# Down weights with 14 adjacent rows in each partition, gate and up read at step 14 to match, in a four-block decode kernel

## The chip, the cores and the metric

The kernel runs on one core of a Trainium2 chip, as one launch. The metric is device time in microseconds. Engines are named as the profile names them: PE is TensorE (matmuls), PEld its loads of the stationary operand, DVE is VectorE, ACT ScalarE, POOL GpSimd, SP SyncE, whose queue issues nearly all transfers here.

## The reference

One token for each of four batch rows passes through attention, a feed-forward block, and the same two again with the same weights. Sizes: model width 512, 32 query heads and 8 key and value heads of width 128, 4096 cached positions, hidden width F = 1792 = 14 x 128, all in bf16.

```python
def _A_ref(x, k_cache, v_cache, wq, wo):
    q = (x @ wq) split into heads
    p = softmax(q . k * Dh ** -0.5)
    return (p . v, heads joined) @ wo

def _B_ref(x, w_gate, w_up, w_down):
    return (_gelu(x @ w_gate) * (x @ w_up)) @ w_down

x = x + _A_ref(_layernorm(x), A_k_cache, A_v_cache, A_wq, A_wo)
x = x + _B_ref(_layernorm(x), B_w_gate, B_w_up, B_w_down)
x = x + _A_ref(_layernorm(x), A_k_cache, A_v_cache, A_wq, A_wo)
x = x + _B_ref(_layernorm(x), B_w_gate, B_w_up, B_w_down)
```

(The first function is cut to what it computes.) The hidden vector of 1792 is summed over in the last product, so any order of its elements gives the same result as long as gate, up and down use the same one.

## The kernel before, in words

All weights stay in SBUF. `load_rest` (L139) loads them once, on SyncE's queue: the output weights `wo_sb` in four parts, gate `wg_sb` and up `wu_sb` in one DMA each, down `wd_sb` in three (L147, chunks 0 to 5, 6 to 10 and 11 to 13). The model dimension lies on the partitions in gate and up, four blocks of 128 (`KD`), each with 1792 columns side by side. The hidden dimension lies on the partitions in down, 14 chunks (`KF`): hidden element c x 128 + p is in partition p, chunk c, so each run of memory that a DMA reads for a partition is one row of 512 bf16, 1 KB.

The order of the work is written out by hand. Batch rows follow one another. For each row, `attend` (or `attend_first`) runs the first layer's attention, and interleaves it with the second layer's attention of the row before. Then `dense` (`dense_first` for row 0, L1109) does the row's first feed-forward block, and after it the queries for its second attention are made. All four rows' second feed-forward block comes at the end, in `dense_last` (L1157). Keys are loaded into fixed tiles, by `load` and `load_pairs` (L472, L481), once the scores that read the tile before are done; values go through a ring of eight slots (`pump`, L634), each loaded again when TensorE has used it. One V tile is 512 KB. In `dense`, `prev.fill()` puts the use of one such V tile of the row before between the matrix products; TensorE works in the order of the program, so what stands behind a product waits for it.

Gate and up are multiplied in three ways:

- `dense_first` calls `ffn_in` (L387): the weights are the stationary operand, 56 blocks of 128 x 128 for each matrix (14 chunks by 4 blocks of the model dimension), and the vector streams past them. They pass through the helper `mac` (L246). `busy(n)` (L443) adds n filler matmuls of 512 columns on `wg_sb`, whose results nobody reads: six between gate and up, four after up, two at each boundary between parts of the down weights. The down product is L246 again, 56 matmuls.
- `dense` calls `ffn_rows` (L289), which goes through `streamed` and `streamed_part` (L274): the vector is the stationary operand, 32 equal columns, and the weights stream past it. Each of the four blocks is cut into four quarters j of 14 x 32 columns, whose results go to PSUM partitions 32j to 32j + 31: 16 matmuls of 448 columns for each matrix. `turn_rows` (L280) then transposes 32 x 32 blocks on VectorE, after which hidden element c x 128 + 32j + n stands in partition 32j + n, column c.
- `dense_last` does the same with the four rows' vectors as stationary operand (`rows_of`, L1166), for gate and then for up. The results are transposed (L1211 and L1216), shifted, scaled (L1212, L1213, with the root from GpSimd in L181), passed through GELU and multiplied (L1215, L1217, L1219); 56 matmuls with the down weights follow (L1205), then the sum with the residual (L1228) and four small DMAs out (L1232).

The pattern that cuts the columns into quarters is the same in both streamed ways:

```python
blocks = w.rearrange("p (c j n) -> p j c n", j=QD, n=QS)
```

with QD = 4 and QS = 32, so the inner 32 columns n are adjacent in memory. `streamed` is also used for the queries (16 matmuls of 512 columns) and for the down product (56 of 128).

Of the kernel before, what the change touches and what calls it, by code (L numbers as in the profile page):

```python
# [15 lines left out]
P = 128  # L16

LN_EPS = 1e-5
QD = 4
QS = P // QD  # L20
# [13 lines left out]
def kernel(  # L34
# [21 lines left out]
    KD = D // P  # L56
    KF = F // P
# [42 lines left out]
    xb = state.tile([P, KD, 2 * RUN], BF16, name="xb")  # L100
# [18 lines left out]
    def acc(shape, name):  # L119
        t = ps_ac.tile([P, 512], FP32, name=name, tag="acc")  # L120
        n = 1
        for s in shape:
            n *= s
        if len(shape) == 1:
            return t[:, :n]
        return t[:, :n].rearrange("p (a b) -> p a b", b=shape[1])

    def wide(v):
        n = v.shape[-1]
        return v.unsqueeze(1).broadcast_to([P, WIDE // n, n])  # L130
# [8 lines left out]
    def load_rest():  # L139
        n = Hq // 4  # L140
        for i in range(4):
            dq.dma_start(out=wo_sb[:, i * n:(i + 1) * n], in_=wo_dram[:, i * n:(i + 1) * n])  # L142
        dq.dma_start(out=wg_sb[:], in_=B_w_gate.rearrange("(k p) n -> p k n", p=P))  # L143
        dq.dma_start(out=wu_sb[:], in_=B_w_up.rearrange("(k p) n -> p k n", p=P))
        wd_dram = B_w_down.rearrange("(k p) n -> p k n", p=P)
        for lo, hi in zip(WD_PARTS, WD_PARTS[1:]):
            dq.dma_start(out=wd_sb[:, lo:hi], in_=wd_dram[:, lo:hi])  # L147

# [17 lines left out]
    def apart(w_sb, shape, at=0):  # L166
        n = shape[0] * shape[1]
        return (w_sb[:, at].bitcast(FP32)[:, :n].rearrange("p (a b) -> p a b", b=shape[1]))

    def stats(b0, nb):  # L170
        st = ps_sm.tile([P, nb, 2], FP32, name="st", tag="sm")
        for i in range(nb):
            b = b0 + i
            for k in range(KD):
                nc.tensor.matmul(st[:, i], lhsT=xb[:, k, b:b + 1].broadcast_to([P, P]),
                                 rhs=xb[:, k, b:B + 1:B - b],
                                 start=k == 0, stop=k == KD - 1, skip_group_check=True)
        return st
# [66 lines left out]
    def mac(dst, lhsT, rhs, first, last):  # L245
        nc.tensor.matmul(dst, lhsT=lhsT, rhs=rhs, start=first, stop=last, skip_group_check=True)  # L246
# [11 lines left out]
                mac(q[:, i], wq_sb[g][:, k, i * Dh:(i + 1) * Dh],  # L258
                    rhs(k) if nb > 1 else wide(rhs(k)), k == 0, k == KD - 1)

    def streamed(name, n, steps):


        full = acc([n, WIDE], name)
        streamed_part(full, steps, range(len(steps)))
        return full

    def streamed_part(full, steps, part):
        flat = full.rearrange("p c r -> p (c r)")
        for i in part:  # L270
            x, w = steps[i]
            blocks = w.rearrange("p (c j n) -> p j c n", j=QD, n=QS)
            for j in range(QD):
                nc.tensor.matmul(flat[j * QS:(j + 1) * QS], lhsT=x.broadcast_to([P, WIDE]),  # L274
                                 rhs=blocks[:, j], start=i == 0, stop=i == len(steps) - 1,
                                 skip_group_check=True)
# [10 lines left out]
        return streamed("q", HG, q_steps(b, g))  # L287

    def ffn_rows(b, w_sb, name):  # L289
        return streamed(name, KF, [(xb[:, k, b:b + 1], w_sb[:, k]) for k in range(KD)])  # L290

    def down_rows(H_bf):
        return streamed("y2", KD, [(H_bf[:, c, :1], wd_sb[:, c]) for c in range(KF)])
# [35 lines left out]
    def nothing(t):  # L329
        nc.scalar.copy(out=t, in_=qb[:, 0:1].broadcast_to([P, t.shape[1]]))  # L330
# [46 lines left out]
    def add_x(b0, nb, y):  # L377
        bs = slice(b0, b0 + nb)
        nc.vector.tensor_tensor(out=xb[:, :, bs], in0=XX[:, bs].rearrange("p b k -> p k b"),  # L379
                                in1=y, op=ALU.add)  # L380
# [6 lines left out]
    def ffn_in(rhs, w_sb, name):  # L387
        g = acc([KF, WIDE], name)
        for c in range(KF):
            for k in range(KD):  # L390
                mac(g[:, c], w_sb[:, k, c * P:(c + 1) * P], wide(rhs(k)), k == 0, k == KD - 1)
        return g

    def shifts(scr, mr, i):
# [762 lines left out]
    def dense_last(y, full):  # L1157
        up = acc([KF, WIDE], "u")
        nothing(up.rearrange("p c r -> p (c r)"))

        def rows_of(w_sb, full):
            flat = full.rearrange("p c r -> p (c r)")
            for k in range(KD):
                blocks = w_sb[:, k].rearrange("p (c j n) -> p j c n", j=QD, n=QS)
                for j in range(QD):
                    nc.tensor.matmul(flat[j * QS:j * QS + B], lhsT=xb[:, k, :B],  # L1166
                                     rhs=blocks[:, j], start=k == 0, stop=k == KD - 1,
                                     skip_group_check=True)
            return flat

        add_x(0, B, y)
        st = stats(0, B)
        add_y(0, B, y)
        ss, mean = st[:, :, 0], st[:, :, 1]
        shape = [KF, B]
        ln = small.tile([P, 3, B], FP32, name="ln", tag="ln")
        msq, own, rstd = ln[:, 0], ln[:, 1], ln[:, 2]
        t = [apart(wq_sb[0], shape, i) for i in range(2)]

        def shift(i):  # L1180
            nc.vector.tensor_tensor(out=t[i], in0=cols(cs_f[:, i], KF, B), in1=rows(mean, KF, B),
                                    op=ALU.mult)

        xlo = wq_sb[1][:, 0, :KD * B].rearrange("p (k b) -> p k b", b=B)
        nc.vector.tensor_tensor(out=xlo, in0=XX.rearrange("p b k -> p k b"),
                                in1=xb[:, :, :B], op=ALU.subtract)
        nc.scalar.activation(out=msq, in_=mean, func=ACT.Square)
        nc.vector.tensor_scalar(out=rstd, in0=ss, scalar1=1.0 / D, scalar2=LN_EPS,
                                op0=ALU.mult, op1=ALU.add)
        shift(0)  # L1190
        nc.vector.tensor_tensor(out=rstd, in0=rstd, in1=msq, op=ALU.subtract)
        inv_root(rstd, rstd)
        shift(1)

        g_rows = rows_of(wg_sb, full)
        u_rows = rows_of(wu_sb, up)
        xr = ps_sm.tile([P, P], FP32, name="xr", tag="sm")
        yo = ps_sc.tile([P, P], FP32, name="yo", tag="sc")
        zero = qb[:, 0:1].broadcast_to([P, P])
        for clear in (xr, yo):  # L1200
            nc.tensor.matmul(clear[:], lhsT=zero, rhs=zero, start=True, stop=True,
                             skip_group_check=True)

        def row(to, k, lhsT, rhs):
            nc.tensor.matmul(to[k * QS:k * QS + B], lhsT=lhsT, rhs=rhs, start=False, stop=True,  # L1205
                             skip_group_check=True)

        for x in (xb[:], xlo):
            for k in range(KD):
                row(xr, k, x[:, k, :B], ident_bf[:])  # L1210
        nc.vector.transpose(out=g_rows, in_=g_rows)  # L1211
        nc.vector.tensor_tensor(out=t[0], in0=full[:, :, :B], in1=t[0], op=ALU.subtract)  # L1212
        nc.vector.tensor_tensor(out=t[0], in0=t[0], in1=rows(rstd, KF, B), op=ALU.mult)  # L1213
        sq = apart(wq_sb[0], shape, 2)
        nc.scalar.activation(out=sq, in_=t[0], func=ACT.Gelu_apprx_tanh)  # L1215
        nc.vector.transpose(out=u_rows, in_=u_rows)  # L1216
        nc.vector.tensor_tensor(out=t[1], in0=up[:, :, :B], in1=t[1], op=ALU.subtract)  # L1217
        H_bf = wq_sb[1][:, 1, :KF * B].rearrange("p (c b) -> p c b", b=B)
        nc.vector.tensor_tensor(out=H_bf, in0=t[1], in1=sq, op=ALU.mult)  # L1219
        nc.vector.scalar_tensor_tensor(out=msq, in0=rstd, scalar=1.0, in1=hmask, op0=ALU.mult,  # L1220
                                       op1=ALU.mult, accum_out=own[:, :1])
        xs = apart(wq_sb[0], [1, P], 3)[:, 0]
        nc.scalar.copy(out=xs, in_=xr[:])
        for c in range(KF):
            for k in range(KD):
                row(yo, k, H_bf[:, c, :], wd_sb[:, c, k * P:(k + 1) * P])
        xo = pep.tile([P, P], BF16, name="xo", tag="pe")
        nc.vector.scalar_tensor_tensor(out=xo[:], in0=yo[:], scalar=own[:, :1], in1=xs,  # L1228
                                       op0=ALU.mult, op1=ALU.add)
        rows_out = out.flatten_outer_dims()  # L1230
        for k in range(KD):
            (nc.sync, nc.scalar)[k % 2].dma_start(out=rows_out[:, k * P:(k + 1) * P],  # L1232
                                                  in_=xo[k * QS:k * QS + B, :])
# [8 lines left out]
    for b in range(B):  # L1242
# [21 lines left out]
        else:  # L1264
            if b == B - 1:
# [7 lines left out]
                rest, steps = acc([HG, WIDE], "q"), q_steps(b, gy)  # L1273
# [33 lines left out]
        else:  # L1307
            y, full = attend_last(q_bf, norm, prev, late[3 * NT:])
# [32 lines left out]
```

## Time and profile before

| what | value |
|---|---|
| time, median of 3 runs | 275.38 us (273.44 to 275.9) |
| profiled execution, its own time | 271.11 us |
| its span, first to last instruction | 269.2 us |
| mean granted TensorE clock | 0.854 |
| busy: PE, DVE, ACT | 190.0, 174.7, 64.2 us |
| bytes moved | 103.08 MB, 102.50 of them from HBM |
| L274 gate and up, 128x448, 48 matmuls each | 3.6 and 2.8 us busy |
| L1166 gate and up, 128x448, 16 matmuls each | 0.9 us busy each |
| L246 gate and up, 56 matmuls each | 1.7 and 1.6 us busy |

The profile records one execution. Matmuls overlap: the duration of one includes its way through the array, so a group's time in the timeline, from its first start to its last end, says more than a mean times a count. The granted clock is the share of full speed that TensorE was given in a stretch. The chain of work that ended last runs back from the last instruction through what released each step.

### The profile page before, as it was taken

What the parts mean: (1) busy time and instruction counts of PE and PEld (TensorE: products, weight loads), DVE (VectorE), ACT (ScalarE), POOL (GpSimd) and SP (SyncE); (2) the same over time, 40 slices, a digit from 0 to 9 for tenths busy, and PEclk for the clock granted to TensorE, in tenths of its full rate; (3) what the DMA queues carried; (4) which work ended last, traced back from release to release, by engine and by line L of the source; (5) the groups of instructions that cost most, each with busy time, mean ns of one, the idle gap of its engine ahead of it and who ended that gap; (6) DMA issues with size and microseconds to landing.
All of it is one profiled execution on the core that took longest, in us unless ns stands there. A gap on an engine that the chain in (4) does not pass through costs nothing.

```text
span 269.2 us, 8883 instructions
## 1 busy us (share of the span) xinstructions
PE 190.0 (71%) x3943; PEld 113.8 (42%) x3943; DVE 174.7 (65%) x428; ACT 64.2 (24%) x125; POOL 2.7 (1%) x8
## 2 busy tenths in 40 slices
PE   1395255634597896968869969687788786788893
PEld 1333133633364443544426335454354354453561
DVE  3394952130124799875676999566759995768863
ACT  1001000100404412030422610304137113044640
POOL 2000000000000000000000000000000000000001
PEclk9999559555599798687897997889979979799999
DMA  6999999999993999999999999999999999999940
GB/s 244 421 417 421 418 420 416 413 382 402 411 360 100 419 415 418 420 418 416 402 386 417 417 420 417 416 422 416 412 417 415 417 419 417 416 391 386 417 159 3
DMA packets 32430, 103.08 MB, mean 383 GB/s; under 512 B 2692, under 2 KB 8584, under 8 KB 32392
## 3 DMA queue, kind: packets, MB, share of 16 engines
q1 hardware_dynamic: 32368, 102.51, 95.1%
q8 instruction: 31, 0.51, 0.7%
q14 instruction: 7, 0.06, 0.1%
q10 hardware_dynamic: 24, 0.01, 0.0%
HBM read 102.50 MB, written 0.00 MB: 381 GB/s over the span
## 4 chain that ended last, share of the span: by engine, by line
DMA 51%; DVE 21%; PE 17%; SPq 6%; issue 2%; ACT 1%; DVEq 0%; ACTq 0%
DMA v_t<-in_A_v_cache_dram 29%; DMA kp<-in_A_k_cache_dram 13%; DVE kp L488 10%; PE sc L531 7%; DMA wu_sb<-in_B_w_up_dram 5%; DMA kp<-in_A_v_cache_dram 4%; SPq L142 4%; PE so L712 2%; DVE pe L541 2%; DVE q L280 2%; DVE qb L316 1%; PE ot L779 1%; PE y L246 1%; PE q L274 1%; SPq L143 1%
## 5 line engine op out<-in xcount | busy, mean ns | idle before, releaser
L488 DVE STREAM_TRANSPOSE kp<-kp 128x1024 f32<-128x1024 f32 x64 | 74.0, 1206 | 0.2 <-issue 0.2
L531 PE MATMUL sc<-kp,qb 128*32 128x512 bf16 x512 | 66.6, 449 | 7.5 <-DVE qb L316 2.5
L779 PE MATMUL ot<-pe,v_t 128*128 128x32 bf16 x1120 | 35.3, 181 | 14.4 <-DMA v_t<-in_A_v_cache_dram 12.4
L779 PEld LDWEIGHTS <-v_t 128*128 128x128 bf16 x1120 | 33.1, 99 | 24.2 <-DMA v_t<-in_A_v_cache_dram 15.9
L531 PEld LDWEIGHTS <-qb 128*32 128x32 bf16 x512 | 21.3, 102 | 42.2 <-issue 23.1
L553 ACT ACTIVATE pe<-sc,nl 128x512 bf16<-128x512 f32 x8 | 5.5, 687 | 84.9 <-DVE pe L550 67.2
L583 PE MATMUL x<-pe,ident_bf 128*32 128x128 bf16 x192 | 6.0, 255 | 15.1 <-DVE pe L561 15.0
L583 PEld LDWEIGHTS <-ident_bf 128*32 128x32 bf16 x256 | 5.6, 107 | 18.9 <-issue 17.1
L541 DVE TENSOR_REDUCE pe<-sc 128x1 f32<-128x512 f32 x12 | 8.3, 689 | 7.9 <-PE sc L531 7.9
L720 DVE STREAM_TRANSPOSE so<-so 128x256 f32<-128x256 f32 (+1 forms) x19 | 11.1, 584 | 3.2 <-PE so L712 3.1
L712 PE MATMUL so<-v_t,pe 128*32 128x256 bf16 x192 | 10.2, 341 | 2.8 <-ACT pe L586 1.4
L246 PE MATMUL y<-OT_bf,wo_sb 128*128 128x32 bf16 x192 | 7.3, 190 | 6.8 <-DMA wo_sb<-in_A_wo_dram 6.7
L246 PEld LDWEIGHTS <-wo_sb 128*128 128x128 bf16 x256 | 8.6, 102 | 8.0 <-DMA wo_sb<-in_A_wo_dram 7.1
L586 ACT CAST pe<-x 128x512 bf16<-128x512 f32 x12 | 7.0, 585 | 20.3 <-PE x L583 20.3
L712 PE MATMUL so<-v_t,pl 128*32 128x256 bf16 x192 | 9.7, 283 | 2.9 <-DMA v_t<-in_A_v_cache_dram 2.6
L379 DVE TENSOR_TENSOR xb<-XX,y 128x4 bf16<-128x4 f32 (+1 forms) x9 | 1.6, 173 | 14.2 <-PE y L246 14.1
L246 PE MATMUL q<-xb,wq_sb 128*128 128x5 bf16 (+1 forms) x192 | 5.4, 170 | 7.3 <-DMA wq_sb<-in_A_wq_dram 7.3
L561 DVE STREAM_TRANSPOSE pe<-pe 128x512 bf16<-128x512 bf16 x12 | 8.4, 697 | 3.2 <-ACT pe L553 3.2
L616 DVE TENSOR_TENSOR OT_bf<-ot,rden 128x8 bf16<-128x8 f32 (+1 forms) x20 | 3.0, 156 | 11.1 <-PE ot L779 11.0
L360 PE MATMUL yr<-wo_sb,OT_bf 128*2 128x512 bf16 (+1 forms) x96 | 10.2, 494 | 0.0
L310 PE MATMUL qe<-q_bf,ident_bf 128*32 128x16 bf16 x256 | 4.4, 175 | 8.2 <-DVE q_bf L299 6.3
L712 PEld LDWEIGHTS <-pe 128*32 128x32 bf16 x208 | 6.1, 113 | 8.2 <-issue 3.8
(148 smaller groups left out, 229.6 us busy)
## 6 DMA issues: line engine op xcount, KB each, us to landing
v_t<-in_A_v_cache_dram SPq DMA_DIRECT2D x97, 512.0 KB, 8.9
kp<-in_A_k_cache_dram SPq DMA_DIRECT2D x40, 512.0 KB, 12.4
kp<-in_A_k_cache_dram SPq DMA_DIRECT2D x12, 1024.0 KB, 8.3
wq_sb<-in_A_wq_dram SPq DMA_DIRECT2D x2, 2048.0 KB
wo_sb<-in_A_wo_dram SPq DMA_DIRECT2D x4, 1024.0 KB, 11.4
wq_sb<-in_A_v_cache_dram SPq DMA_DIRECT2D x3, 1024.0 KB, 11.2
wg_sb<-in_B_w_gate_dram SPq DMA_DIRECT2D x1, 1792.0 KB
wu_sb<-in_B_w_up_dram SPq DMA_DIRECT2D x1, 1792.0 KB
```

The source lines that it names most:

```text
L142: dq.dma_start(out=wo_sb[:, i * n:(i + 1) * n], in_=wo_dram[:, i * n:(i + 1) * n])
L246: nc.tensor.matmul(dst, lhsT=lhsT, rhs=rhs, start=first, stop=last, skip_group_check=True)
L360: nc.tensor.matmul(self.rows[j:j + x.shape[1]], lhsT=x, rhs=wo_sb[:, i], start=self.n < QD, stop=True, skip_group_check=True)
L488: nc.vector.transpose(out=words, in_=words)
L531: nc.tensor.matmul(sc[s * QS:(s + 1) * QS], lhsT=qb[:, w0:w0 + 2 * W], rhs=kt[:, :, be // 2, :, be % 2], start=(t == 0 and be == 0), stop= ...
L541: nc.vector.tensor_reduce(out=m, in_=sc.rearrange("p c j -> p (c j)"), axis=AX.X, op=ALU.min if norm else ALU.max)
L561: nc.vector.transpose(out=flat, in_=flat)
L583: nc.tensor.matmul(x[a * QS:(a + 1) * QS, s], lhsT=ident_bf[:, s * QS:(s + 1) * QS], rhs=pT[:, a], start=True, stop=True, skip_group_check ...
L586: nc.scalar.copy(out=pe, in_=x.rearrange("p s t c h -> p (s t c h)"))
L712: nc.tensor.matmul(ps[d, :NW * QS], lhsT=x[:, w:w + NW].rearrange("p c h -> p (c h)"), rhs=v[:, i:i + NW, d], start=first and i == 0, stop ...
L720: nc.vector.transpose(out=flat, in_=flat)
L779: nc.tensor.matmul(self.ot[:, s % 2], lhsT=v[:, i, :], rhs=wide(pe[:, s, t * CH + i, :]), start=(done == 0 and i == 0), stop=(done == NT - ...
```

## The change

Down is read so that partition p holds the 14 adjacent rows 14p to 14p + 13; chunk c is row 14p + c. One partition's part of a load is then one run of memory of 6, 5 or 3 KB, in place of as many separate rows of 1 KB. The three DMAs and their bytes stay.

Gate and up are loaded as before. Their columns are read in the matching order: hidden element 14p + c must come out in partition p, column c. In `ffn_in` the block of 128 columns becomes every fourteenth column from c on; in `streamed_part` and `rows_of` a quarter is 32 x 14 adjacent columns, and the stream takes the inner 32 at a step of 14 (28 bytes). The queries and the down product keep the old order. Numbers and sizes of matmuls, and everything after them, are the same.

```diff
-        wd_dram = B_w_down.rearrange("(k p) n -> p k n", p=P)
+        wd_dram = B_w_down.rearrange("(p k) n -> p k n", p=P)
         for lo, hi in zip(WD_PARTS, WD_PARTS[1:]):
             dq.dma_start(out=wd_sb[:, lo:hi], in_=wd_dram[:, lo:hi])
...
-    def streamed(name, n, steps):
+    in_chunks = dict(order="p (c j n) -> p j c n", j=QD, n=QS)
+    in_rows = dict(order="p (j n c) -> p j c n", j=QD, n=QS)
+
+    def blocks_of(w, order, **sizes):
+        return w.rearrange(order, **sizes)
+
+    def streamed(name, n, steps, layout=in_chunks):
         full = acc([n, WIDE], name)
-        streamed_part(full, steps, range(len(steps)))
+        streamed_part(full, steps, range(len(steps)), layout)
         return full
 
-    def streamed_part(full, steps, part):
+    def streamed_part(full, steps, part, layout=in_chunks):
         flat = full.rearrange("p c r -> p (c r)")
         for i in part:
             x, w = steps[i]
-            blocks = w.rearrange("p (c j n) -> p j c n", j=QD, n=QS)
+            blocks = blocks_of(w, **layout)
             for j in range(QD):
                 nc.tensor.matmul(flat[j * QS:(j + 1) * QS], lhsT=x.broadcast_to([P, WIDE]),
                                  rhs=blocks[:, j], start=i == 0, stop=i == len(steps) - 1,
...
     def ffn_rows(b, w_sb, name):
-        return streamed(name, KF, [(xb[:, k, b:b + 1], w_sb[:, k]) for k in range(KD)])
+        return streamed(name, KF, [(xb[:, k, b:b + 1], w_sb[:, k]) for k in range(KD)], in_rows)
...
         for c in range(KF):
             for k in range(KD):
-                mac(g[:, c], w_sb[:, k, c * P:(c + 1) * P], wide(rhs(k)), k == 0, k == KD - 1)
+                mac(g[:, c], w_sb[:, k, c::KF], wide(rhs(k)), k == 0, k == KD - 1)
         return g
...
             for k in range(KD):
-                blocks = w_sb[:, k].rearrange("p (c j n) -> p j c n", j=QD, n=QS)
+                blocks = blocks_of(w_sb[:, k], **in_rows)
                 for j in range(QD):
                     nc.tensor.matmul(flat[j * QS:j * QS + B], lhsT=xb[:, k, :B],
```

## The prediction

> **What bounds the kernel now.** I read the page's rate row first, then the chain of work that ended last, then single stretches by windows and by timeline. The rate row gives the GB/s of 40 slices of 6.73 us.
>
> ```profile
> GB/s 244 421 417 421 418 420 416 413 382 402 411 360 100 419 415 418 420 418 416 402 386 417 417 420 417 416 422 416 412 417 415 417 419 417 416 391 386 417 159 3
> ...
> DMA 51%; DVE 21%; PE 17%; SPq 6%; issue 2%; ACT 1%; DVEq 0%; ACTq 0%
> ```
>
> Nearly every slice is at 416 to 421, so bytes set the time: 102.5 MB at 417 GB/s are 246 us of the span of 269.2. The rest is the hole in slice 13 and the last ten microseconds, where no transfer is left. Only there does a slower engine lengthen the run one for one. The hole, by windows of 2 us (last two columns: share of the DMA engines, GB/s):
>
> ```profile
> 59.00:61.00 2.00, 1.06 (x32) 1.07 (x32) 0.00 (x0) 0.00 (x0) 0.00 (x0) 0.50 1.09 386
> 67.00:69.00 2.00, 0.00 (x0) 0.00 (x0) 0.54 (x3) 1.45 (x3) 0.00 (x0) 0.50 1.02 416
> 75.00:77.00 2.00, 1.94 (x47) 1.20 (x43) 0.72 (x4) 0.00 (x0) 0.00 (x0) 1.00 1.06 370
> ...
> 83.00:85.00 2.00, 2.00 (x36) 1.09 (x40) 0.05 (x1) 0.86 (x1) 0.00 (x0) 1.00 0.00 0
> ```
>
> The windows at 59 and 75 carry the output and down weights, rows of 1 KB: 370 to 386 GB/s. The window at 67 carries gate, rows of 3.5 KB: 416. At 83 nothing moves. The chain shows what closes the hole:
>
> ```profile
> 60.01 14.43 DMA wu_sb<-in_B_w_up_dram
> 74.48 1.60 PE u L246 x56
> ...
> 76.85 0.23 DVE words L433
> 77.22 0.75 PE y L246 x24
> ...
> 82.99 2.10 PE sc L531 x27
> ```
>
> It is a run of computation from the landing of up to the first scores. SyncE's next load waits for those (L481 for PE sc L531, once for 10.5 us in its waits). In the timeline, the matmuls that the change makes stepped (start, duration, then what):
>
> ```profile
> 127.57 1.69 PE L274 MATMUL g<-wg_sb,xb 128*32 128x448 bf16 x16
> ...
> 237.41 0.94 PE L274 MATMUL g<-wg_sb,xb 128*32 128x448 bf16 x16
> ```
> ```profile
> 261.67 0.93 PE L1166 MATMUL gr<-wg_sb,xb 128*4 128x448 bf16 x16
> ...
> 262.43 0.93 PE L1166 MATMUL u<-wu_sb,xb 128*4 128x448 bf16 x16
> ...
> 262.65 0.67 DVE L1211 STREAM_TRANSPOSE gr<-gr 128x448 f32<-128x448 f32 x1 [0.19 <-PE gr L1166]
> ...
> 263.67 0.22 DVE L1213 TENSOR_TENSOR wq_sb<-wq_sb,ln 128x56 f32<-128x56 f32 x1
> 263.80 0.66 DVE L1216 STREAM_TRANSPOSE u<-u 128x448 f32<-128x448 f32 x1
> ```
>
> Sixteen go as four rounds of four column quarters running together. At granted clock 1.00 up starts 0.76 us after gate, so a round takes 190 ns. The group at 127.57 ran at 0.50: less the 0.58 us of its last matmul, 1.69 us are three rounds of 370 ns. The group at 261.67 stands in the open tail.
>
> **The change, part by part.** The sum is made on the profiled execution, 271.11 us (span 269.2, 1.9 around it). It lies 1.6% under the median of 275.38 and below the lowest of the three runs, 273.44; I add the difference to the median.
>
> *Down weights loaded (L147).* 1.835 MB in rows of 6, 5 and 3 KB in place of 1 KB; three DMAs as before. At 416 in place of 370 to 386 GB/s they take 4.4 us, not 4.8 to 5.0: 0.4 to 0.6 us sooner. Who waits? The timeline has the last twelve L246 matmuls on them at 79.25, 0.07 us behind the filler ahead of them (two L443 matmuls of 0.22 us from 78.75); the first 24 start 0.14 us after L433 ends. So at most 0.15 us is on the chain. The 1 MB of K behind them lands sooner into a hole whose end is set by scores. SyncE gets through L147 sooner and then stands in L481's wait; nothing is issued sooner. Price: -0.1, between -0.6 (all of it on the path) and 0.
>
> *Gate and up as weights at step 14 (L391, first row of the batch).* Twice 56 loads of 128x128. They run at 27 ns each at 70.15 (1.68 us, granted clock 0.50) and at 26 at 74.48 (1.58 us, 1.00). So they don't follow the array's clock, and a read that only reached half speed would be hidden at full clock. Lower end 0. Upper end: the slowest 128x128 load in the trace, the f32 one of L566, 188 ns against 96 in its own row; twice the pace would be 1.5 us for each matrix. Both are on the chain into the hole: gate's ends at 71.84, six fillers run to 74.39, up lands then. No slack, so +2.9. I take +0.1, by the pair at 70.15 and 74.48, which is the same instruction.
>
> [...] No run here shows a step of 14 in a weight load.
>
> *Gate and up as streams at step 14, rows two to four (L274).* Neighbouring elements lie 28 bytes apart. No row of before reads that way. The nearest stepped row is the scores' (L531, step 2): 32 matmuls of 512 in 2.00 us at 245.65, against 1.05 for 16 unit-step ones (L274 q). Less the last matmul (0.39 and 0.38) these are seven rounds of 230 ns and three of 223: 3%. From there to step 14 I have bounds only. Lower: no cost, 190 ns a round. Upper: the four quarters no longer run together. One stream of 512 takes 0.22 us in the L443 fillers (four in 1.02 us with the drain), so a quarter of 448 takes 188 and a round 750 ns, four times. Between lies a read at half speed, as the group at 127.57 shows it: 370 ns, twice. I take twice. Step 2 already costs a little where a read with speed to spare would cost nothing, which speaks against zero; that quarters would queue behind one another is something the unit-step rows, four abreast, give no sign of.
>
> At twice, each matrix takes 0.75 us more: 1.5 us in each of three rows of the batch. TensorE is in order, so V tiles behind it are consumed and their slots reissued later. The cover is the queue: a V tile issued at 127.49 lands 5.7 us later (chain), one at 232.60 after 7.84. So 1.5 us leave the DMAs fed. Yet the windows around 132 to 139 sag to 356 to 401 GB/s with the queue at its shortest, so I put +0.2 there for all three. If the cover were gone it would be 3 x 1.5 = +4.5.
>
> *The same in the tail (L1166).* Gate's last result comes 0.75 us later and the vector chain from L1211 on moves with it: L1216 from 263.80 to 264.55. Up starts 0.75 later and takes 0.75 more: its end goes from 263.36 to 264.86, past 264.55, so L1216 starts at about 264.9. Cost +1.1. At four times: 263.36 + 4.5 = 267.86, so +4.1. At no cost 0.
>
> Sum: -0.1 + 0.1 + 0.2 + 1.1 = +1.3 us; 271.1 becomes 272.4, and the median 276.7.
>
> [...]
>
> **The rivals.** *No penalty.* Stepping streams for nothing leaves -0.1: 275.3 us. For it: only 3% at step 2.
>
> *Quarters take turns* (the other side: slower). Four times a round: tail +4.1; in each middle row 2 x 2.2 = 4.5 us, against a cover of 5.7. The reissues at 237 to 242 would come just as the queue runs out, about 1 us lost per row, so +3; loads +0 to +2.9. Together +7 to +10, middle 283.9. It decides from about three times on, where the tail alone gives 263.36 + 3.0 - 263.8 = +2.6. For it: four streams each touching a new place on every element. Against: no row has it.
>
> *The weight loads slow down, streams or not.* 1.5 to 2.9 us in the hole with twice the pace, above that if they fall to the pace of L566, 131 ns (two matmuls in 0.39 us at 228.00, the second 0.26 of it), which is 56 x 105 ns = +5.9 for each matrix: 277 to 287. Against: the pace's indifference to the clock.
>
> *Half speed, but the cover fails*: +1.3 and up to +4.3, 278 to 281. *Faster*: the whole down load on the path is 0.6 us, 0.2%; more than 1% would need something the trace does not show.
>
> **How the numbers follow.** About 1%, 2.75 us, is what a measurement of this kernel can tell from no change. Half speed 0.38 (276.7) and no penalty 0.20 (275.3) are within it: 0.58. Turns 0.24, slow weight loads 0.10 and the failed cover 0.05 are slower: 0.39. Faster 0.03. The likeliest one's own range is 275.5 to 278. The range goes down to 274.0, no penalty with the scatter of the runs, and up to the middle of the turns at 284.0; left out are the upper half of the turns (0.12), the top of the loads (0.04) and faster (0.03).
>
> **What would show it.** In the tail, L1166 at 1.7 us for each matrix at clock 1.00: half speed; 0.93 no penalty; 3.2 turns. L1216 should follow the end of up, not L1213. L246 on gate and up in the hole should stay near 1.6 us. The down weights' windows should read near 416 GB/s with the hole wider on its early side. The slices around 135 and 240 tell whether the cover held. I am wrong if the tail's length doesn't move, or if the hole ends later than 11 us after up's landing.

## The result and the profile after

The changed kernel takes 291.59 us (median of 6 runs, 290.24 to 293.11), the one before 274.01 us in the same count of runs (271.82 to 275.9). The ratio is 1.0676, 95% interval 1.0635 to 1.0717: 18.5 us slower. (It is taken over fast runs alone, so it is not quite the quotient of these medians.) I had forecast 276.7 with 284.0 as the upper end. The profiled execution after took 290.24 us, its span 288.4.

The rate row and the shares of the chain of work that ended last, after:

```profile
GB/s 260 419 419 419 419 419 417 392 392 418 412 33 255 417 420 417 417 418 358 272 383 414 418 419 418 417 370 292 366 412 417 419 418 418 369 276 345 332 3 3
...
DMA 41%; PE 27%; DVE 23%; SPq 4%; issue 2%; ACT 2%; DVEq 0%
```

A slice is now 7.21 us. Before there was one hole and a tail; now there are three further dips (358 272 383, then 370 292 366, then 369 276 345), one for each of batch rows two to four. In the chain, transfers fell from 51% to 41% and TensorE rose from 17% to 27%. Timeline of the hole after (start, duration, what, and the idle time before it; the view ends at 81 us, inside the last two groups):

```profile
69.92 3.55 PE L246 MATMUL g<-xb,wg_sb 128*128 128x32 bf16 x56 [2.80 <-DMA wg_sb<-in_B_w_gate_dram]
...
75.83 3.51 PE L246 MATMUL u<-xb,wu_sb 128*128 128x32 bf16 x56
...
80.47 0.63 PEld L246 LDWEIGHTS <-wd_sb 128*128 128x128 bf16 x22 [0.75 <-issue]
80.50 0.68 PE L246 MATMUL y<-words,wd_sb 128*128 128x32 bf16 x21 [0.28 <-DVE words L439]
```

The stepped weight loads take 3.55 and 3.51 us for a matrix in place of 1.68 and 1.58. Gate's run pushes the fillers past the landing of up, up starts 1.35 us late, and the down product starts 3.28 us later than before (77.22 to 80.50). It no longer waits for its weights: its last twelve matmuls start 0.43 us after the two fillers ahead of them (82.03 to 82.46), in place of 0.50 (78.75 to 79.25). The first scores, which end the hole, start 3.20 us later (82.99 to 86.19). The first middle row, by timeline and by windows of 1 us:

```profile
130.66 3.42 PE L280 MATMUL g<-wg_sb,xb 128*32 128x448 bf16 x16
...
134.28 3.47 PE L280 MATMUL u<-wu_sb,xb 128*32 128x448 bf16 x16
```
```profile
134.00:135.00 1.00, 1.00 (x16) 0.37 (x12) 0.85 (x2) 0.00 (x0) 0.00 (x0) 0.58 0.63 250
135.00:136.00 1.00, 1.00 (x12) 0.25 (x8) 0.05 (x1) 0.84 (x2) 0.00 (x0) 1.00 0.61 217
137.00:138.00 1.00, 1.00 (x20) 0.38 (x12) 0.22 (x1) 0.00 (x0) 0.00 (x0) 1.00 0.10 41
138.00:139.00 1.00, 0.19 (x8) 0.00 (x0) 0.86 (x4) 0.00 (x0) 0.00 (x0) 1.00 0.06 20
```

A product that took 0.94 us at full clock takes 3.4. Less its last matmul (about 0.99) these are three rounds of 810 ns. The first product ran mostly at granted clock 0.50 (0.61 over its length) and the second mostly at 1.00 (0.92), and both take the same. The transfers run dry behind them, down to 20 GB/s. The tail after:

```profile
276.15 3.43 PE L1172 MATMUL gr<-wg_sb,xb 128*4 128x448 bf16 x16
...
279.37 3.44 PE L1172 MATMUL u<-wu_sb,xb 128*4 128x448 bf16 x16
...
279.62 0.67 DVE L1217 STREAM_TRANSPOSE gr<-gr 128x448 f32<-128x448 f32 x1 [2.67 <-PE gr L1172]
...
282.84 0.67 DVE L1222 STREAM_TRANSPOSE u<-u 128x448 f32<-128x448 f32 x1 [1.99 <-PE u L1172]
```

The second transpose now waits 1.99 us for the end of up. From the first gate matmul to the issue of the output it is 9.41 us (276.15 to 285.56), where it was 4.85 (261.67 to 266.52): +4.56.

### The profile page after: what moved, and what is told of

It is laid out like the page before. It is cut to its first block, busy times and chain, and to the rows that moved or that the text cites. A ratio compares the mean times of both kernels' runs of the same rounds, so it can differ in the third digit from the quotient of the medians.

```text
span 288.4 us, 8883 instructions
## 1 busy us (share of the span) xinstructions
PE 208.7 (72%) x3943; PEld 118.4 (41%) x3943; DVE 174.7 (61%) x428; ACT 64.4 (22%) x125; POOL 2.7 (1%) x8
## 2 busy tenths in 40 slices
DMA packets 31022, 103.08 MB, mean 357 GB/s; under 512 B 2692, under 2 KB 6792, under 8 KB 30984
## 4 chain that ended last, share of the span: by engine, by line
DMA 41%; PE 27%; DVE 23%; SPq 4%; issue 2%; ACT 2%; DVEq 0%
DMA v_t<-in_A_v_cache_dram 20%; DMA kp<-in_A_k_cache_dram 16%; DVE kp L494 9%; DMA wg_sb<-in_B_w_gate_dram 4%; SPq L142 4%; PE g L280 3%; PE u L280 3%; PE sc L537 3%; PE ot L785 2%; PE so L718 2%; PE y L246 2%; DVE q L286 1%; DVE pe L547 1%; PE idle L449 1%; PE yr L366 1%
## 5 line engine op out<-in xcount | busy, mean ns | idle before, releaser
L537 PE MATMUL sc<-kp,qb 128*32 128x512 bf16 x512 | 62.6, 430 | 7.3 <-DVE qb L322 2.5
L718 PE MATMUL so<-v_t,pe 128*32 128x256 bf16 x192 | 10.8, 350 | 3.2 <-DMA v_t<-in_A_v_cache_dram 2.2
L280 PEld LDWEIGHTS <-xb 128*32 128x32 bf16 x208 | 5.8, 103 | 11.2 <-issue 8.0
L280 PE MATMUL u<-wu_sb,xb 128*32 128x448 bf16 x48 | 10.3, 988 | 0.0
L280 PE MATMUL g<-wg_sb,xb 128*32 128x448 bf16 x48 | 10.3, 986 | 0.0
```

The costliest lines, as they stand in the source:

```text
L537: nc.tensor.matmul(sc[s * QS:(s + 1) * QS], lhsT=qb[:, w0:w0 + 2 * W], rhs=kt[:, :, be // 2, :, be % 2], start=(t == 0 and be == 0), stop= ...
L718: nc.tensor.matmul(ps[d, :NW * QS], lhsT=x[:, w:w + NW].rearrange("p c h -> p (c h)"), rhs=v[:, i:i + NW, d], start=first and i == 0, stop ...
```

## The experiments

A number such as 1.0147 below is the ratio to the kernel before on the same chip, with its 95% interval; microseconds from it are taken on that kernel's 273.1 to 273.9 us.

**One part at a time.** Four kernels divide the change.

```diff
# tail_only, in rows_of alone
-                blocks = w_sb[:, k].rearrange("p (c j n) -> p j c n", j=QD, n=QS)
+                blocks = w_sb[:, k].rearrange("p (j n c) -> p j c n", j=QD, n=QS)
# first_only, in ffn_in alone
-                mac(g[:, c], w_sb[:, k, c * P:(c + 1) * P], wide(rhs(k)), k == 0, k == KD - 1)
+                mac(g[:, c], w_sb[:, k, c::KF], wide(rhs(k)), k == 0, k == KD - 1)
# down_only, in load_rest alone
-        wd_dram = B_w_down.rearrange("(k p) n -> p k n", p=P)
+        wd_dram = B_w_down.rearrange("(p k) n -> p k n", p=P)
# middle_only: the change's streamed, streamed_part and ffn_rows, all else as before
```

> Before, with the step of 14 only in the last feed-forward block (the output is then not the reference's, since the order of the hidden elements no longer matches down's). Theory of the two traces: the tail grows by 4.4 us (first gate matmul to the output's issue: 4.9 us before, 9.4 after) and nothing else moves: 278.4 us against 274.0. Rival, that the tail costs little and the middle rows most: under 2 us.

> Before, with the step of 14 only in the streamed products of batch rows two to four (the order then doesn't match down's). If the queue of V tiles does not cover them: each product takes 2.5 us longer, 5.0 us a row, of which the two traces lost about 3.8 in the DMAs: +11 us in all, 285. If my cover of 4 to 5.7 us held: +3 at most, 277.

> Before, with the step of 14 only in the weight loads of batch row one (the order then doesn't match down's). By the changed trace the loads take 60 ns in place of 26, 1.9 us for each matrix, and the hole in the transfers ends 3.3 us later: 277.3 us. If the hole had slack for gate's part: +1.9. If the loads were hidden: 0.

> Before, with only the down weights loaded as 14 adjacent rows in each partition (gate and up keep their order, so the products don't match). My prediction and the changed trace, where the last twelve down matmuls start without a wait: the load is 0.4 to 0.6 us shorter and 0.1 of it is on the path, so 0 to -0.2 us, not to be told from no change. Rival, the shorter load moves everything behind it: -0.6, 0.2%. Nothing should make it slower.

Measured: tail 1.0147 (1.0098 to 1.0196), +4.0 us; middle 1.0409 (1.0349 to 1.0469), +11.2; first 1.0154 (1.0086 to 1.0221), +4.2; down 0.9965 (0.9931 to 0.9999), -1.0, between -1.9 and 0. The four add up to 18.4, the change's 18.5, with an uncertainty of about 3 us in the sum. So each part acts where the traces show it, and the middle rows cost most. The 4.2 of the first row is the least certain: in that run's trace the first scores start 3.37 us later (86.36), and its tail, which it leaves as it was, ran at granted clock 0.50, so some of the 4.2 may be the clock's. The down load alone is a small gain; its interval holds my 0.1 and the rival's 0.6 alike, so how much is left open. Two of its windows of 2 us show the faster rows:

```profile
74.00:76.00 2.00, 1.62 (x57) 1.52 (x58) 0.01 (x1) 0.00 (x0) 0.00 (x0) 1.00 1.00 408
76.00:78.00 2.00, 1.72 (x30) 1.00 (x29) 0.78 (x4) 0.00 (x0) 0.00 (x0) 1.00 1.04 422
```

The same two windows of the kernel before read 381 and 398. The next one, 78 to 80, falls from 375 to 296, as the hole opens earlier.

**The price of a step.** Matmuls appended behind the end of the kernel before, read from the gate weights.

```diff
+        def streams(name, step, width, rounds=6):
+            t = acc([256], name)
+            for i in range(rounds):
+                for j in range(width):
+                    nc.tensor.matmul(t[j * QS:(j + 1) * QS], lhsT=x, rhs=read(256, step, j), ...)
+        def weights(name, step, count=16):
+            t = acc([QS], name)
+            for i in range(count):
+                nc.tensor.matmul(t, lhsT=read(P, step, i % 3), rhs=x, ...)
```

> The kernel before, with matmuls appended behind its end whose results nobody reads: streams of 256 bf16 columns of the gate weights at steps 1 to 16, four column quarters abreast (six rounds each), alone (twelve) and in pairs, and loads of 128 columns at steps 1 to 14 as the stationary operand. Changed trace: four abreast at step 14 take 800 ns a round for 448 columns, 1.79 ns an element. Theory A, the cost follows the number of 16-byte stretches touched, 1.79 ns each for every stream: rounds of 256 take 109 ns at step 1, 115 at 2, 172 at 3, 229 at 4, 286 at 5, 344 at 6, 401 at 7, 458 at 8 and no more beyond it; loads take 26 ns at steps 1 and 2, 30 at 4, 53 at 7, 60 at 8 and 14. Theory B, a threshold: 109 at every step below 8, 458 from 8 on. Theory C, any step but 1 and 2 costs the full 458. Who shares the limit: if all streams share it, a stream alone at step 14 takes 115 ns and a pair 229; if each has its own, both take 458. [...]

The timeline of this kernel's end; the tile's name gives the number of streams and the step:

```profile
266.40 0.83 PE L1247 MATMUL abreast_one<-wg_sb,qb 128*32 128x256 bf16 x24
267.05 0.85 PE L1247 MATMUL abreast_two<-wg_sb,qb 128*32 128x256 bf16 x24
...
268.76 1.56 PE L1247 MATMUL abreast_four<-wg_sb,qb 128*32 128x256 bf16 x24
...
276.29 2.92 PE L1247 MATMUL abreast_eight<-wg_sb,qb 128*32 128x256 bf16 x24
...
287.28 2.99 PE L1247 MATMUL abreast_sixteen<-wg_sb,qb 128*32 128x256 bf16 x24
290.04 1.49 PE L1247 MATMUL alone_one<-wg_sb,qb 128*32 128x256 bf16 x12
...
300.18 5.59 PE L1247 MATMUL alone_eight<-wg_sb,qb 128*32 128x256 bf16 x12
...
315.19 0.57 PE L1253 MATMUL load_one<-qb,wg_sb 128*128 128x32 bf16 x16
...
318.37 1.11 PE L1253 MATMUL load_fourteen<-qb,wg_sb 128*128 128x32 bf16 x16
```

From one group's start to the next there are six rounds abreast: 2.71 us from the start of eight to that of ten (279.00 in the same view) are 452 ns a round. By the starts of single matmuls in the trace, rounds take 109 ns at step 1, 114 at 2, 171 at 3, 229 at 4, 285 at 5, 340 at 6, 402 at 7, 452 at 8, 464 at 14 and 460 at 16, all at granted clock 1.00. Theory A fits at every step: from step 2 on, 1.78 ns for each 16-byte stretch that a stream touches, up to one element a stretch. That the stretch has 16 bytes was a supposition when the theory was set up; the rounds show it, as they grow up to step 8, 16 bytes from one element to the next, and hardly beyond (452 ns there, 464 at 14, 460 at 16). B and C fall. One stream alone takes 109, 114, 226, 396, 451 and 457 ns at steps 1, 2, 4, 7, 8 and 14, a pair at 14 457, where four abreast take 464: the limit is each stream's own, and quarters don't queue behind one another. The loads follow the same order: 25 ns each at steps 1 and 2, 32 at 4, 54 at 7, 61 at 8 and 60 at 14.

A second set of appended matmuls asks whether it is the stretch or the jump that costs, and what a step on the write side does.

```diff
+        def grouped(k, step):
+            return lambda j: (w[:, j * 1000:j * 1000 + 256 // k * step]
+                              .rearrange("p (n s) -> p n s", s=step)[:, :, :k])
+        def written(step):
+            return lambda t: t[:, :127 * step + 1:step]
```

> Before, with other matmuls appended behind its end whose results nobody reads. Reads of 256 columns, four abreast, of 1, 2, 4 or 8 adjacent elements out of every 16, and of 2 or 4 out of every 8. If the cost is 1.78 ns for each 16-byte stretch touched (as the appended streams at steps 1 to 16 gave), rounds take 456, 228, 114 and 109 ns for the sixteens, and 228 and 114 for the eights. If a jump in itself costs, whatever lies beside it, two of eight (a jump of 12 bytes) would come out cheaper than two of sixteen; if only the innermost step counts, all but the first take 109. Writes: adjacent reads of 128 columns, written to PSUM at steps 1 to 4, four abreast and alone. The kernel that writes at a step of 32 took 376 ns for 448 columns where 189 is plain, at granted clock 1.00: about 56 ns a round at step 1 and 107 at any other step, abreast and alone, if each write that leaves its neighbour out takes two beats; more at larger steps if the writes pay by distance.

```profile
268.72 0.83 PE L1247 MATMUL in_plain<-wg_sb,qb 128*32 128x256 bf16 x24
269.38 2.93 PE L1247 MATMUL in_one_of_sixteen<-wg_sb,qb 128*32 128x256 bf16 x24
272.12 1.58 PE L1247 MATMUL in_two_of_sixteen<-wg_sb,qb 128*32 128x256 bf16 x24
273.51 0.88 PE L1247 MATMUL in_four_of_sixteen<-wg_sb,qb 128*32 128x256 bf16 x24
...
276.92 0.53 PE L1247 MATMUL out_plain<-wg_sb,qb 128*32 128x128 bf16 x24
277.25 0.85 PE L1247 MATMUL out_two<-wg_sb,qb 128*32 128x128 bf16 x24
```

Rounds of 460, 232, 114 and 109 ns for 1, 2, 4 and 8 of sixteen, 227 and 114 for 2 and 4 of eight. The number of stretches decides; how far the jump goes does not (232 ns for two of sixteen, 227 for two of eight). Four elements out of each stretch (here, or at step 2) are nearly free, 114 ns where 109 is plain; two cost double, 227 to 232. Writes: 56 ns a round at step 1 and 109 at steps 2, 3 and 4 abreast, and at 2 and 4 alone.

**The step on the write side in the whole kernel.**

```diff
+    in_rows = dict(order="p (j n c) -> p j n c", j=QD, n=QS)
...
+            to = flat if layout is in_chunks else full.rearrange("p c r -> p r c")
...
-                nc.tensor.matmul(flat[j * QS:(j + 1) * QS], lhsT=x.broadcast_to([P, WIDE]),
+                nc.tensor.matmul(to[j * QS:(j + 1) * QS], lhsT=x.broadcast_to([P, WIDE]),
```

> The change, with the streamed products reading gate and up in adjacent columns and writing them to PSUM at a step of 32 elements instead (the same result in the same place); batch row one still loads weights at step 14. If writes at a step are free, the tail and the middle rows are as before and only the hole's +4 us stays: 278. [...]

1.0347 (1.0292 to 1.0403): +9.5 us. The timeline has a first middle row at mostly half clock and then at full:

```profile
131.66 2.77 PE L281 MATMUL g<-wg_sb,xb 128*32 128x448 bf16 x16
...
134.48 1.67 PE L281 MATMUL u<-wu_sb,xb 128*32 128x448 bf16 x16
```

The 278 for free writes is not met: a write at a step halves the pace, at either clock (rounds of 747 ns against 373 at 0.50, 376 against 189 at 1.00). It costs less than the stepped read, whose rounds are 810 ns. Of 9.5 us about 4.2 are the weight loads, which this kernel keeps. It halves the loss and stays behind the kernel before.

**A step of 2.** Two adjacent rows of down in each partition, so that gate and up are read at step 2. The down parts end at chunks 6, 10 and 14 here.

```diff
-        wd_dram = B_w_down.rearrange("(p k) n -> p k n", p=P)
+        wd_dram = B_w_down.rearrange("(a p s) n -> p a s n", p=P, s=STEP)
-    in_rows = dict(order="p (j n c) -> p j c n", j=QD, n=QS)
+    in_rows = dict(order="p (a j n s) -> p j a s n", j=QD, n=QS, s=STEP)
```

> The change with two adjacent rows in each partition in place of 14: runs of 2 KB, gate and up at step 2. By the appended streams (114 ns for 256 columns against 109, loads 25 against 25) a round of 448 takes 200 ns in place of 190, 0.04 us a matrix: tail +0.05, hole 0, middle covered. With -0.1 of the down load that is no change, within 0.2%. If it is the permuting itself and not the step that costs, it is several us slower.

0.9991 (0.9958 to 1.0024): no change. The same permuting without the long step costs nothing, so it is the step. It gains nothing either. The trace adds a limit to theory A. In the last middle row, at granted clock 1.00 (238.54 to 240.47 us), rounds of the stepped products take 190 ns, as plain ones do, where 1.78 ns for each of 112 stretches would be 199. Here 32 elements are read at step 2, and then their neighbours in the same stretches; why this is free, and the appended streams at step 2 lost 5%, no run shows.

**What binds the middle rows.**

```diff
# middle_gate, on middle_only
+                        in_rows if name == "g" else in_chunks)
# early_fills, on the change, in dense
+        prev.fill()
         g = ffn_rows(b0, wg_sb, "g")
...
         u = ffn_rows(b0, wu_sb, "u")
-        for _ in range(2):
-            prev.fill()
+        prev.fill()
# light_before and light_after, in pump
-                dq.dma_start(out=v, in_=cache_tile(A_v_cache, *key[1:]))
+                c = CH // 2 if key[0] == 2 else CH
+                dq.dma_start(out=v[:, :c], in_=cache_tile(A_v_cache, *key[1:])[:, :c])
```

> The middle rows alone with the step only in gate, not in up (products don't match): 2.5 us of delay a row in place of 5.0, which cost 3.7 a row (284.4 against 273.1). If a fixed cover of about 1.3 us a row stood ahead of the loss: +3.7 in all, 276.8. If nearly nothing is covered and the loss is in proportion: +5.6, 278.7. If the cover is the 4 us of my prediction and breaks only beyond it: under +1, 274.

1.0144 (1.0106 to 1.0183): +3.9 us, between 2.9 and 5.0, where a loss in proportion would be 5.6. Half of the delay costs about a third of the loss: 1.3 of 2.5 us a row get through, and of the second 2.5 nearly all (11.2 - 3.9 = 7.3 of 7.5). The cover was about 1.2 us a row (0.8 to 1.5), not 4.

> The whole change, with two of the V tiles that rows two to four use between the products used one product earlier (one ahead of gate, one ahead of up), so that their slots are reissued 3.4 us sooner; the result is the same. If the middle rows lose their time because slots come free late and the transfers run dry (134 to 140 us in the changed trace: 250, 217, 348, 41, 20, 291 GB/s), two tiles of 1.25 us each fill the gap: 4 to 7 us less than the change's 291.6, 285 to 288. If the middle rows are bound by the chain of computation itself, through queries, scores and key transposes, and the dry transfers only follow from it: no gain, 291 or a little more.

1.0821 (1.0753 to 1.089) where the change has 1.0676: about 4 us slower than the change, not 4 to 7 faster. The theory of late slots had forecast the opposite. The timeline shows what the earlier use did:

```profile
132.25 0.62 PE L718 MATMUL so<-v_t,pl 128*32 128x256 bf16 x8 [0.46 <-DMA v_t<-in_A_v_cache_dram]
```

TensorE waited 0.46 us for the tile, and gate (at 132.63) began that much and the use itself later. About 1 us a row put ahead of gate came out as some 1.3 us a row at the end, as it would if the chain of computation sets the pace. That the chain sets it was the rival; a run with fewer bytes tests it.

> The kernel before, with only the first half of each V tile that the second layer's attention takes through the ring loaded (the other half holds old data, so the output is not the reference's): 11 tiles a row, 256 KB less each, 2.9 MB or 6.9 us of transfer a row less. Theory C, the middle rows' chain of computation is only some 1.2 us a row shorter than their transfers (the cover that middle_gate and middle_only left): 3 to 5 us less, about 269.5. Theory D, transfers alone bind and the chain is far from it: 15 to 20 us less, 255.

> The same half loads in the changed kernel. Theory C, the chain binds its middle rows (58 us from one row's queries to the next's, against 54.5 before) and the dry transfers follow from it: 0 to 2 us less than the change, 290 to 291.6. Theory D, late slots starve the transfers, so that fewer bytes help as much as before: 10 us less or more, 280.

Both moved 94.43 MB in place of 103.08. Light before: 0.9943 (0.9908 to 0.9978), -1.6 us. Light after: 1.071 (1.0623 to 1.0796), the change's 1.0676 within the intervals: nothing gained. Their rate rows, before and after, and after it the shares of the chain that ended last:

```profile
GB/s 245 420 417 422 416 421 418 412 382 401 412 370 94 410 416 418 421 418 385 214 292 391 418 420 417 417 382 207 253 399 414 418 418 421 404 171 264 400 75 3
```
```profile
GB/s 258 420 419 419 419 419 419 389 394 421 393 17 254 419 417 417 417 409 102 177 318 419 417 419 419 411 139 160 289 422 411 421 417 413 162 145 335 284 3 3
...
DMA 39%; PE 29%; DVE 23%; SPq 4%; issue 2%; ACT 2%; DVEq 0%; ACTq 0%
```

With 8.6 MB less to move, some 21 us at 417 GB/s, the DMAs simply stand idle longer in the same three places. So there, around the feed-forward block of each middle row, the chain of computation sets the pace of the changed kernel, and the dry transfers follow from it: D falls. Before the change that chain was already within about half a microsecond a row of the transfers (1.6 us over three rows, between 0.6 and 2.5, where theory C had forecast 3 to 5).

This holds for those stretches, not for whole rows. Between 94.5 and 129.5 us the light changed kernel still moves 418 GB/s, and its chain of work goes from one landing to the next (9.9, 9.9 and 8.8 us); between 129.5 and 152 us it moves 204. DMA keeps 39% of the chain. Only V tiles of the second layer were made smaller; no run here takes bytes from the other loads.

The kernel before had shown how short its cover was. The prediction named two V tiles by the time from issue to landing, one issued at 127.49 us and one at 232.60. TensorE uses them here (the idle time before each use is in brackets):

```profile
133.23 0.40 PE L712 MATMUL so<-v_t,pl 128*32 128x256 bf16 x8 [0.26 <-DMA v_t<-in_A_v_cache_dram]
...
240.48 0.40 PE L712 MATMUL so<-v_t,pl 128*32 128x256 bf16 x8 [0.84 <-DMA v_t<-in_A_v_cache_dram]
```

It was ready only 0.26 and 0.84 us before they landed, and in the row between it waited 0.95 and 0.54 us. In that execution, this is all by which the gate and up products could have been later without TensorE coming late for its tile.

## Why the prediction was wrong, point by point

Term by term, forecast and then measured: down load -0.1 and -1.0 us, weight loads +0.1 and +4.2, middle rows +0.2 and +11.2, tail +1.1 and +4.0.

- **The size of the stream's penalty.** This is the step that failed first: "Between lies a read at half speed ... I take twice." It is 4.3 times: rounds of 810 ns where 190 are plain. My upper end of 750 was nearly the right number for a wrong reason, four quarters taking turns. The runs show each stream alone paying 1.78 ns for every 16-byte stretch. The row that I had set aside pointed there: four elements a stretch at 1.78 ns are 0.45 ns an element, against 0.42 for a plain stream (190 ns for 448), a loss of 5% where I read 3% at step 2. If such a limit is behind the 3%, it leaves no room at all, and step 8 and beyond must cost four times. That is read afterwards, and the row alone could not have settled it: in step_two's own products a step of 2 cost nothing.
- **Weight loads.** Taken as +0.1, measured +4.2 (2.3 to 6.0), with the hole's end 3.20 us later in the changed trace. The argument "they don't follow the array's clock" was true and led the wrong way: it showed that something other than the clock sets a plain load's pace (27 ns at granted clock 0.50, 26 at 1.00), not that a slower read would be hidden. The upper end I had set, twice the pace and +2.9, was close: 60 ns against 26. The sign that I had named came true: up's weights were being loaded at 75.41, so up had landed by then, and the scores that end the hole run to 88.25, more than 11 us later. The lower end of 0 does not hold: the appended loads took 60 ns at step 14 against 25 at step 1. By what means a step slows a load, no run shows.
- **The middle rows' cover.** "The cover is the queue ... 5.7 us." I read it from the landing time of a V tile and concluded that bytes set the time. A full rate row shows that the DMAs are busy, not that computation has time to spare. How long a tile takes to land says nothing of that either; how long TensorE waits for it does, and for these two tiles that was 0.26 and 0.84 us. The light runs put the cover at about 0.5 us a row, middle_gate at about 1.2. So 5.0 us of delay a row cost 3.7, and the middle rows are 11 of the 18.5 us. Both steps made this miss: with the right size and my cover I had +3, in the rival at four times, so by that estimate about 8 of the 11 are the cover's.
- **The tail.** The mechanism held: L1222, the transpose of up, follows the end of up. The products took 3.43 us in place of the 1.7 that I had named for half speed. At four times I had worked out +4.1; measured +4.0 as a kernel, +4.56 in the trace.
- **The down load.** Right in sign and in being small: the down product no longer waits, the rate in two windows rose from 381 and 398 to 408 and 422, and in that run the hole widens on its early side. -1.0 us, between -1.9 and 0, against my -0.1.
- **Rivals.** Turns (283.9) had nearly the right size for the stream, but not the cause: one stream alone at step 14 takes as long as four abreast (457 and 464 ns). The slow weight loads (277 to 287) were true besides. I had treated these as alternatives; one change of step made both happen together.

## What to carry to other kernels

Before a stream or a weight load is given a step, count the 16-byte stretches that it will touch: up to 4 bytes from one bf16 element to the next was nearly free here (114 ns a round where 109 is plain, loads 25 and 25), 16 bytes and more cost over four times in a stream (452 to 464) and over twice in a weight load (60 and 61). A transfer made better where hardly anything waits for it cannot pay for that: -1.0 us here. A saturated rate row says nothing of slack elsewhere. Look how long the engine waits for each tile, or take bytes away in an experiment: where the time then hardly falls (here by 1.6 us for 8.6 MB less), the chain of computation is as long as the transfers.

## What the runs showed of the hardware that was not expected

- A stepped read does not depend on the granted clock: the change's gate products took 3.42 us at 1.00 (from 188.94 us) and 3.44 at 0.52 (from 247.57 us). A stepped write to PSUM does: at step 32 rounds of 747 ns at 0.50 and 376 at 1.00 (plain 373 and 189). At 1.00, steps 2, 3 and 4 double the time as well (109 against 56 ns); at 0.50 only step 32 was run.
- The limit on reads belongs to the single stream: four streams abreast at step 14 moved four times the elements of one in much the same time, 464 ns a round against 457.
- A load of 128 stationary columns at step 14 takes 60 ns, 0.47 ns a column, a quarter of a stream's 1.78 for an element. Why a load pays less, no run here shows.
- The tail can run at either clock: where the profile of first_only has it at 0.50, its unchanged tail products took 1.66 and 1.71 us in place of 0.93.
